# Two PSUM accumulator tiles for the second matmul in place of one, in a convolution and gated MLP kernel

## The chip, the cores and the metric

The kernel runs on one core of a Trainium2 chip. The metric is the device time of one execution in microseconds (us). The runs of the kernel before took 2665.88 to 2666.84 us, median 2666.54.

## What is computed

An input of 8 x 4096 tokens with 192 channels goes through a causal convolution of 7 taps (one softmax-normalised set of taps for each of 8 heads), and each token then through an MLP of width 2048 whose activation is a ratio of a cubic and a quadratic polynomial. Cut to what matters:

```python
# convolution: w = softmax(weight) over the 7 taps, per head
x_unf = x_pad[:, idx, :].reshape(B, S, K, H, group)
x = np.einsum('hk,bskhg->bshg', w, x_unf).reshape(B * S, D)
# MLP
h = x @ w_in                                   # 192 -> 2048
P = a[0] + a[1] * h + a[2] * h**2 + a[3] * h**3
Q = 1.0 + np.abs(b[0]) * np.abs(h) + np.abs(b[1]) * h**2
out = (P / (Q + 1e-6)) @ w_out                 # 2048 -> 192
```

## The kernel before

The 32768 tokens are cut into 64 **chunks** of 512 tokens. Each chunk passes through 8 **units**; unit k computes 256 of the 2048 hidden columns for the chunk's 512 tokens. So there are 512 units.

For a unit, PE runs gemm1 (line 512): ten matmuls of 512 columns into a PSUM tile `hp` (two buffers). ACT and DVE turn `hp` into the activation: on ACT the steps A (line 583, writes A from hp), B (586, A in place), t (579, from hp), l (593, a logarithm) and y (597, an exponential); on DVE four operations of line 305, here told apart by what they write and read: t<-t,cf,hp; g<-t,cf,y; A<-A,cf,y; g<-A,cf,g. The last leaves the unit's activation `g` in SBUF. Then PE runs gemm2 (line 521), which multiplies `g` with `w_out` and accumulates over the eight units of a chunk into PSUM. In the trace each of gemm2's fp32 matmuls is two pieces, so that a unit's gemm2 is 16 rows "op".

gemm2 comes in two **pairs**: pair 0 holds tokens 0 to 255 of the chunk, pair 1 tokens 256 to 511, each as two groups of 128. Its target is one tile `op` of [128, 4, 256] fp32, from a pool of one buffer. It is 4 KiB a partition; pair 0 writes the first 2 KiB and pair 1 the second. When a chunk's last unit is in, ACT copies the sums out in two steps of line 530 (`ob`, one for each pair), and SP sends each to memory (533).

The order of PE, ACT, DVE and POOL is written out beforehand by a planner (`plan`): a list of tasks with costs, dependencies and ranks. On PE it is gemm1 of unit k, then gemm2 of unit k-3, pair 0 and then pair 1. In the planner the first gemm2 of a chunk depends, for each pair, on the eviction of the same pair of the chunk before. The semaphore waits do not come from the planner. They are made from what each instruction reads and writes, tile by tile, and from when a pool's buffer is free again.

POOL computes the convolution of later chunks: tap by tap it scales a shifted input and adds it with an accumulating DMA; each step is tied to the end of one unit's last DVE step. The first two chunks take their convolution from PE instead. The kernel has two bodies for two kinds of coefficients; the one called with `fast` true runs here.

Of the kernel before, what the change touches and what calls it, by code (L numbers as in the profile page):

```python
# [10 lines left out]
F32 = mybir.dt.float32  # L11
# [9 lines left out]
NB, S, D = 8, 4096, 192  # L21
# [3 lines left out]
P = 128  # L25
# [179 lines left out]
def kernel(  # L205
# [13 lines left out]
    nc = tc.nc  # L219
# [12 lines left out]
    ps_o = ctx.enter_context(tc.tile_pool(name="ps_o", bufs=1, space=PS))  # L232
# [135 lines left out]
    wo_t = const.tile([P, FT, D], F32, name="wo_t")  # L368
# [8 lines left out]
    def body(fast):  # L377
# [37 lines left out]
        CP, TMP, X, H, G, O, st, last_step = {}, {}, {}, {}, {}, {}, {}, {}  # L415
# [97 lines left out]

        def gemm2(k, pair):
            c, i = divmod(k, UPC)
            if i == 0 and pair == 0:
                O[c] = ps_o.tile([P, 4, 256], F32, name="op")
            for j in range(2):
                f = 2 * i + j
                for t in (2 * pair, 2 * pair + 1):  # L520
                    nc.tensor.matmul(O[c][:, t, 0:D], lhsT=G[k][:, j, t * P:t * P + P], rhs=wo_t[:, f, :],  # L521
                                     start=(f == 0 and t % 2 == 0), stop=(f == FT - 1 and t % 2 == 1))
            if pair == 1:
                del G[k]

        def out_evac(c, pair):
            ob = opool.tile([P, 2, D], F32, name="ob")
            o = O[c][:, 2 * pair:2 * pair + 2, 0:D]
            if fast:
                nc.scalar.activation(out=ob, in_=o, func=AF.Copy, scale=K["rO"])  # L530
            else:
                nc.scalar.copy(out=ob, in_=o)
            nc.sync.dma_start(out=out_v[c, pair], in_=ob)
            if pair == 1:
                del O[c]

        def flat(t):
            return t.rearrange("p a b -> p (a b)")
# [72 lines left out]
        with tc.manual_schedule(engines={E.PE, E.Activation, E.DVE, E.Pool}):  # L611
            for kind, *which in plan(fast):
                {"w": prep, "c": conv, "xh": conv_high, "xl": conv_low, "g1": gemm1, "g2": gemm2,
                 "O": out_evac, "x": tap, "a": tap_add, "t": tap_weights, "h": high, "l": low_part}.get(kind, partial(unit, kind))(*which)
# [65 lines left out]
```

## Time and profile before

| | us |
|---|---|
| median of 3 runs | 2666.54 |
| profiled execution, its own time | 2666.89 |
| span from the first to the last instruction in it | 2664.7 |
| PE busy | 2534.2 (95%) |
| ACT busy | 2539.2 (95%) |
| DVE busy | 2516.9 (94%) |
| POOL busy | 1235.7 (46%) |
| mean granted TensorE clock | 0.995 of full speed |

Three engines are busy for nearly the whole span. A busy share is an average over the span and does not say which engine the others follow. For that one reads the chain that ended last, and then one short stretch engine by engine. A row of a timeline gives the start, the duration, the engine and line, what is written and read, and in brackets the idle time of that engine just before and what released it. An operation may start before the end of the one ahead of it on the same engine, since their first and last parts overlap.

### The profile page before, as it was taken

The page shows a single profiled execution, that of the slowest core. Times are in us where ns is not written, and L with a number is a line of the kernel's source. Part 1 is how long each engine was busy: PE and PEld are TensorE (multiplying, and loading weights), DVE is VectorE, ACT ScalarE, POOL GpSimd, SP SyncE. Part 2 cuts the span into 40 slices and gives each one's busy share as a digit, 9 for nine tenths or more (in the row PEclk, how much of TensorE's full clock was granted, in tenths as well). Part 3 has the DMA queues.
Part 4 walks back from the last instruction along what each step waited for, and adds up shares of the span by engine and source line. Part 5 has one row for each costly group of instructions (what it writes and reads, how often), then busy time and mean ns, then how long its engine had stood idle before and what let it go on. Part 6 is the DMA issues. An engine that isn't in the chain of part 4 may idle for free.

```text
span 2664.7 us, 35994 instructions
## 1 busy us (share of the span) xinstructions
PE 2534.2 (95%) x13528; PEld 2299.1 (86%) x13528; DVE 2516.9 (94%) x2160; ACT 2539.2 (95%) x2739; POOL 1235.7 (46%) x1452
## 2 busy tenths in 40 slices
PE   5999999999999999999999999999999999999998
PEld 4888888888888888888888888888888888888887
DVE  8999999999999999999999999999999999999998
ACT  7999999999999999999999999999999999999997
POOL 4454454544544444545445445454454444454530
PEclk8999999999999999999999999999999999999999
DMA  5445444445444444444544544444444444444430
GB/s 156 99 98 107 101 100 99 97 104 104 92 105 101 99 103 102 98 105 93 107 96 97 107 102 99 99 97 103 104 94 104 102 98 103 102 98 104 94 76 14
DMA packets 101721, 263.96 MB, mean 99 GB/s; under 512 B 9760, under 2 KB 44832, under 8 KB 101536
## 3 DMA queue, kind: packets, MB, share of 16 engines
q0 software_dynamic: 53568, 195.06, 38.4%
q1 hardware_dynamic: 47664, 66.04, 8.5%
q8 instruction: 108, 1.77, 0.3%
q14 instruction: 77, 0.63, 0.1%
q10 hardware_dynamic: 304, 0.46, 0.1%
HBM read 41.32 MB, written 25.17 MB: 25 GB/s over the span
## 4 chain that ended last, share of the span: by engine, by line
PE 87%; ACT 8%; DVE 2%; issue 2%; DMA 0%; POOL 0%; SPq 0%; DVEq 0%; ACTq 0%
PE op L521 50%; PE hp L512 38%; ACT l L593 2%; ACT A L586 2%; ACT ob L530 2%; ACT t L579 1%; DVE g L305 1%; DVE A L305 0%; DVE t L305 0%; ACT y L597 0%; DVE wo_t L399 0%; ACT ad L385 0%; ACT A L583 0%; PE y L434 0%; DMA wb_t<-in_wband 0%
## 5 line engine op out<-in xcount | busy, mean ns | idle before, releaser
L521 PE MATMUL op<-wo_t,g 128*128 128x192 f32 x8192 | 1424.4, 327 | 100.9 <-ACT ob L530 90.3
L521 PEld LDWEIGHTS op<-wo_t,g 128*128 128x128 f32 x8192 | 1355.6, 190 | 163.8 <-ACT ob L530 116.4
L512 PE MATMUL hp<-xh,wh_t 128*128 128x512 f32 x2048 | 872.5, 426 | 15.3 <-DVE t L305 10.6
L305 DVE SCALAR_TENSOR_TENSOR g<-t,cf,y 128x1024 f32<-128x1024 f32 x512 | 655.2, 1280 | 95.6 <-ACT y L597 78.9
L305 DVE SCALAR_TENSOR_TENSOR t<-t,cf,hp 128x1024 f32<-128x1024 f32 x512 | 653.9, 1277 | 33.8 <-ACT t L579 33.8
L305 DVE SCALAR_TENSOR_TENSOR g<-A,cf,g 128x1024 f32<-128x1024 f32 x512 | 657.0, 1283 | 1.2
L305 DVE SCALAR_TENSOR_TENSOR A<-A,cf,y 128x1024 f32<-128x1024 f32 x512 | 654.0, 1277 | 0.0
L512 PE MATMUL hp<-xh,wl_t 128*128 128x512 f32 x2048 | 633.5, 391 | 0.0
L583 ACT ACTIVATE A<-hp 128x1024 f32<-128x1024 f32 x512 | 522.1, 1020 | 49.5 <-PE hp L512 33.3
L593 ACT ACTIVATE l<-A 128x1024 f32<-128x1024 f32 x512 | 542.6, 1060 | 6.2
L586 ACT ACTIVATE A<-A 128x1024 f32<-128x1024 f32 x512 | 541.6, 1058 | 0.0
L597 ACT ACTIVATE y<-l 128x1024 f32<-128x1024 f32 x512 | 525.6, 1027 | 4.2 <-DVE xl L499 0.2
L579 ACT ACTIVATE t<-hp 128x1024 f32<-128x1024 f32 x512 | 522.0, 1020 | 0.0
L447 POOL TENSOR_SCALAR tmp<-xt,wt_t,zero 128x512 f32<-128x512 f32 x496 | 377.5, 767 | 209.3 <-DVE g L305 202.6
L512 PEld LDWEIGHTS hp<-xh,wl_t 128*128 128x128 f32 x2048 | 386.1, 189 | 86.7 <-DVE wl_t L407 0.2
L512 PEld LDWEIGHTS hp<-xh,wh_t 128*128 128x128 f32 x2048 | 387.1, 189 | 80.0 <-DVE t L305 7.3
L453 POOL DMA_DIRECT2D acc<-tmp x248 | 214.9, 867 | 414.0 <-DMA acc<-xs 369.1
L512 PE MATMUL hp<-xl,wh_t 128*128 128x512 f32 x1024 | 403.4, 394 | 0.0
L447 POOL TENSOR_SCALAR xs<-xt,wt_t,zero 128x512 f32<-128x512 f32 x248 | 188.7, 767 | 205.8 <-DVE g L305 205.8
L512 PEld LDWEIGHTS hp<-xl,wh_t 128*128 128x128 f32 x1024 | 194.2, 190 | 20.4 <-DVE xl L499 0.3
L473 POOL TENSOR_SCALAR xh<-acc,one,zero 128x1024 fp32r<-128x1024 f32 x62 | 74.2, 1198 | 251.0 <-DVE g L305 245.6
L453 POOL DMA_DIRECT2D acc<-xs x124 | 109.4, 882 | 61.3 <-DMA acc<-tmp 43.1
(57 smaller groups left out, 424.3 us busy)
## 6 DMA issues: line engine op xcount, KB each, us to landing
acc<-tmp POOLq DMA_DIRECT2D x248, 512.0 KB, 4.5
acc<-xs POOLq DMA_DIRECT2D x124, 512.0 KB, 5.2
xt<-in_xt SPq DMA_DIRECT2D x62, 518.0 KB, 4.0
out<-ob SPq DMA_DIRECT2D x128, 192.0 KB, 2.6
raw<-in_w_in SPq DMA_DIRECT2D x8, 512.0 KB, 5.7
raw<-in_w_out SPq DMA_DIRECT2D x8, 384.0 KB, 4.1
xs<-in_xa ACTq DMA_DIRECT2D x1, 324.0 KB, 4.7
xs<-in_xa SPq DMA_DIRECT2D x1, 324.0 KB, 6.5
```

The source lines that it names most:

```text
L305: return nc.vector.scalar_tensor_tensor(out=out_, in0=a, scalar=s, in1=b, op0=op0, op1=op1)
L447: ins = nc.gpsimd.tensor_scalar(to[:, n * CH:n * CH + CH], of[:, n * XA + k:n * XA + k + CH], wt_t[:, n, k:k + 1], zero, ALU.mult, ALU.add)
L453: nc.gpsimd.dma_start(out=CP[c], in_=TMP.pop((c, k)), accum_op=ALU.add)
L473: ins = nc.gpsimd.tensor_scalar(X[c][0].rearrange("p a b -> p (a b)"), CP[c], one, zero, ALU.mult, ALU.add)
L512: nc.tensor.matmul(H[k][:, j, :], lhsT=w[:, i, part, j, :], rhs=x, start=(n == 0), stop=(n == 4))
L521: nc.tensor.matmul(O[c][:, t, 0:D], lhsT=G[k][:, j, t * P:t * P + P], rhs=wo_t[:, f, :], start=(f == 0 and t % 2 == 0), stop=(f == FT - 1 ...
L530: nc.scalar.activation(out=ob, in_=o, func=AF.Copy, scale=K["rO"])
L579: nc.scalar.activation(out=work_tile(k, "t"), in_=h, func=AF.Square, scale=K["rt"], bias=1.0)
L583: nc.scalar.activation(out=work_tile(k, "A"), in_=h, func=AF.Abs, scale=K["rA"])
L586: nc.scalar.activation(out=s["A"], in_=s["A"], func=AF.Square, bias=1.0)
L593: nc.scalar.activation(out=work_tile(k, "l"), in_=s["A"], func=AF.Ln, scale=K["rL"], bias=1.0)
L597: nc.scalar.activation(out=work_tile(k, "y"), in_=s["l"], func=AF.Exp, scale=-1.0)
```

## The change

`op` becomes two tiles, `op0` and `op1`, one for each pair, each of [128, 2, 256] fp32 (2 KiB a partition), and each with one buffer under a name of its own. The matmuls and the two copies on ACT do the same work on the same amount of PSUM.

```diff
         def gemm2(k, pair):
             c, i = divmod(k, UPC)
-            if i == 0 and pair == 0:
-                O[c] = ps_o.tile([P, 4, 256], F32, name="op")
+            if i == 0:
+                O[c, pair] = ps_o.tile([P, 2, 256], F32, name=f"op{pair}")
             for j in range(2):
                 f = 2 * i + j
                 for t in (2 * pair, 2 * pair + 1):
-                    nc.tensor.matmul(O[c][:, t, 0:D], lhsT=G[k][:, j, t * P:t * P + P], rhs=wo_t[:, f, :],
+                    nc.tensor.matmul(O[c, pair][:, t % 2, 0:D], lhsT=G[k][:, j, t * P:t * P + P], rhs=wo_t[:, f, :],
                                      start=(f == 0 and t % 2 == 0), stop=(f == FT - 1 and t % 2 == 1))
...
         def out_evac(c, pair):
             ob = opool.tile([P, 2, D], F32, name="ob")
-            o = O[c][:, 2 * pair:2 * pair + 2, 0:D]
+            o = O.pop((c, pair))[:, :, 0:D]
...
-            if pair == 1:
-                del O[c]
```

The planner is not touched, and no engine's order changes. What changes are the waits of two instructions at each chunk boundary. On ACT, around the two evictions of a chunk (the number behind a name is that of the buffer or tile; `DMAHW` is the transfer that frees `ob`), before:

```order
L583 ACTIVATE A_2609<-hp_2589 128x1024 [waits PE_49]
L597 ACTIVATE y_2613<-l_2602 128x1024 [waits DVE_49,Activation_49]
L530 ACTIVATE ob_2619<-op_2347 128x384 [waits DMAHW2_49,PE_49]
L586 ACTIVATE A_2609<-A_2609 128x1024 [waits Activation_49]
L579 ACTIVATE t_2640<-hp_2589 128x1024
L593 ACTIVATE l_2643<-A_2609 128x1024 [waits Activation_49]
L530 ACTIVATE ob_2651<-op_2347 128x384 [waits DMAHW3_49]
L597 ACTIVATE y_2654<-l_2643 128x1024 [waits DVE_49,Activation_49]
```

and now:

```order
L581 ACTIVATE A_2616<-hp_2596 128x1024 [waits PE_49]
L595 ACTIVATE y_2620<-l_2609 128x1024 [waits DVE_49,Activation_49]
L530 ACTIVATE ob_2626<-op0_2353 128x384 [waits DMAHW2_49,PE_49]
L584 ACTIVATE A_2616<-A_2616 128x1024 [waits Activation_49]
L577 ACTIVATE t_2647<-hp_2596 128x1024
L591 ACTIVATE l_2650<-A_2616 128x1024 [waits Activation_49]
L530 ACTIVATE ob_2658<-op1_2365 128x384 [waits DMAHW3_49,PE_49]
L595 ACTIVATE y_2661<-l_2650 128x1024 [waits DVE_49,Activation_49]
```

Each eviction now reads a tile of its own and waits for PE itself; before, the first waited for PE on behalf of both. On PE, around the first gemm2 of the next chunk, before:

```order
L512 MATMUL hp_2629<-xl_2368,wh_t_182 128x512
L512 MATMUL hp_2629<-xh_2367,wh_t_182 128x512
L512 MATMUL hp_2629<-xh_2367,wl_t_183 128x512 x2
L521 MATMUL op_2646<-wo_t_184,g_2587 128x192 [waits DVE_49,PE_49,Activation_49]
L521 MATMUL op_2646<-wo_t_184,g_2587 128x192 x7
L512 MATMUL hp_2668<-xh_2367,wh_t_182 128x512 [waits DVE_49]
```

and now:

```order
L512 MATMUL hp_2636<-xl_2375,wh_t_182 128x512
L512 MATMUL hp_2636<-xh_2374,wh_t_182 128x512
L512 MATMUL hp_2636<-xh_2374,wl_t_183 128x512 x2
L521 MATMUL op0_2653<-wo_t_184,g_2594 128x192 [waits DVE_49,Activation_49]
L521 MATMUL op0_2653<-wo_t_184,g_2594 128x192 x3
L521 MATMUL op1_2664<-wo_t_184,g_2594 128x192 [waits Activation_49]
L521 MATMUL op1_2664<-wo_t_184,g_2594 128x192 x3
L512 MATMUL hp_2676<-xh_2374,wh_t_182 128x512 [waits DVE_49]
```

The wait for ACT that stood once, ahead of all eight matmuls, stands twice now, ahead of each pair's four.

## Rows read from the trace of the kernel before

**Rows 1.** The page, part 4: the chain that ended last, by engine.

```profile
PE 87%; ACT 8%; DVE 2%; issue 2%; DMA 0%; POOL 0%; SPq 0%; DVEq 0%; ACTq 0%
```

**Rows 2.** Busy time by stretch: one chunk, behind the late boundary at 256, behind a boundary.

```profile
core 0: us, PE busy (x) PEld busy (x) DVE busy (x) ACT busy (x) POOL busy (x), PEclk, DMA share, GB/s
...
1218.73:1259.55 40.82, 39.34 (x210) 35.73 (x209) 38.71 (x33) 39.30 (x43) 19.56 (x24) 1.00 0.48 100
...
258.00:260.30 2.30, 2.30 (x10) 2.30 (x8) 2.30 (x3) 2.30 (x3) 1.55 (x2) 0.51 0.00 0
...
1240.00:1274.00 34.00, 34.00 (x183) 31.14 (x182) 32.42 (x28) 33.00 (x35) 15.87 (x19) 1.00 0.48 94
```

**Rows 3.** The chain in order of time at a chunk boundary: start, us, what.

```profile
1228.79 2.28 PE hp L512 x10
1231.07 2.61 PE op L521 x16
...
1237.43 2.87 PE op L521 x16
1240.30 2.31 PE hp L512 x10
1242.61 2.60 PE op L521 x16
```

**Rows 4.** Waits: total us, times, longest us.

```profile
PE op L521 <- ACT ob L530: 90.3, 62, 2.4
```

**Rows 5.** Timeline of PE at that boundary.

```profile
1230.91 2.76 PE L521 MATMUL op<-wo_t,g 128*128 128x192 f32 x16
1233.37 0.53 PE L512 MATMUL hp<-xh,wh_t 128*128 128x512 f32 x1
...
1237.43 2.87 PE L521 MATMUL op<-wo_t,g 128*128 128x192 f32 x16 [1.48 <-ACT ob L530]
```

**Rows 6.** Timeline of ACT: an early boundary, this boundary, the end of this chunk.

```profile
134.28 1.05 ACT L593 ACTIVATE l<-A 128x1024 f32<-128x1024 f32 x1
135.22 1.02 ACT L583 ACTIVATE A<-hp 128x1024 f32<-128x1024 f32 x1
...
1232.02 1.02 ACT L597 ACTIVATE y<-l 128x1024 f32<-128x1024 f32 x1
1233.70 0.49 ACT L530 ACTIVATE ob<-op 128x384 f32<-128x384 f32 x1 [0.66 <-PE op L521]
...
1236.89 0.49 ACT L530 ACTIVATE ob<-op 128x384 f32<-128x384 f32 x1
1237.26 1.04 ACT L597 ACTIVATE y<-l 128x1024 f32<-128x1024 f32 x1
1238.20 1.03 ACT L583 ACTIVATE A<-hp 128x1024 f32<-128x1024 f32 x1
...
1241.13 1.06 ACT L593 ACTIVATE l<-A 128x1024 f32<-128x1024 f32 x1
1242.64 1.02 ACT L583 ACTIVATE A<-hp 128x1024 f32<-128x1024 f32 x1 [0.45 <-PE hp L512]
...
1270.84 1.06 ACT L593 ACTIVATE l<-A 128x1024 f32<-128x1024 f32 x1
1271.92 1.02 ACT L583 ACTIVATE A<-hp 128x1024 f32<-128x1024 f32 x1
```

**Rows 7.** Timeline of PE and of all engines at two earlier boundaries.

```profile
174.34 2.87 PE L521 MATMUL op<-wo_t,g 128*128 128x192 f32 x16 [0.57 <-ACT ob L530]
...
256.01 4.55 PE L521 MATMUL op<-wo_t,g 128*128 128x192 f32 x16 [2.43 <-ACT ob L530]
```

**Rows 8.** Timeline of ACT at the end of the program.

```profile
2658.62 0.87 ACT L530 ACTIVATE ob<-op 128x384 f32<-128x384 f32 x2 [7.49 <-PE op L521]
```

**Rows 9.** Line 530's instructions on ACT's queue: count, ns min/median/max.

```profile
L530 ACTq EVENT_SEMAPHORE  x63: 17/17/17, 129.0 to 2650.1; - x63
```

**Rows 10.** Timeline of DVE at the boundary.

```profile
1236.09 1.28 DVE L305 SCALAR_TENSOR_TENSOR t<-t,cf,hp 128x1024 f32<-128x1024 f32 x1 [0.53 <-ACT t L579]
...
1244.62 1.28 DVE L305 SCALAR_TENSOR_TENSOR g<-t,cf,y 128x1024 f32<-128x1024 f32 x1 [1.28 <-ACT y L597]
```

## The prediction

> **What bounds the kernel now.** I read the chain of waits first. It says which engine the end hangs on: 87% of the span is TensorE work [rows 1]. Busy shares alone would not tell this, since in one chunk PE, ACT and DVE are busy 39.34, 39.30 and 38.71 of 40.82 us [rows 2]. Then the chain in order of time, around one chunk boundary. Away from the boundary it alternates gemm1 of a unit (hp, 2.28 us) with gemm2 of the unit three earlier (op, 2.60), with nothing between: 4.88 us a unit, and 8 x 4.88 = 39.04 us a chunk. [...] At the boundary the chain leaves PE: op ends at 1233.68, the next op starts only at 1237.43, and what lies between on the chain is ACT [rows 3]. The waits view gives the place: PE waited 62 times for the eviction "ob", 90.3 us in all [rows 4].
>
> Call the new chunk's units 0 to 7 and the evictions of the old chunk O0 (pair 0) and O1 (pair 1). PE's timeline [rows 5]: gemm2 of the old unit 7 from 1230.91, gemm1 of unit 3 from 1233.37, then 1.48 idle, then gemm2 of unit 0 at 1237.43. ACT's timeline [rows 6]: it issues y at 1232.02, then is idle 0.66 waiting for PE, O0 at 1233.70, three steps, O1 at 1236.89 for 0.49, so done at 1237.38. PE goes 0.05 after that. So two waits are in a row: O0 waits for all 16 matmul pieces of the old gemm2 (they end at 1230.91 + 2.76 = 1233.67, and O0 starts 0.03 later), which pushes O1 back, and the new chunk's first matmul waits for O1, though it writes only pair 0's half.
>
> **What the change does to O0.** It has to wait for pair 0's 8 pieces only. These end half of 2.60 before the others, at about 1233.67 - 1.30 = 1232.37. ACT has its queue slot after y: an op behind y starts 0.94 after it (1237.26 to 1238.20 [rows 6]), so O0 goes at 1232.96, now bound by ACT's own order and not by PE. Gain on ACT: 0.74, and everything queued behind O0 moves up with it, O1 to 1236.15, done at 1236.64.
>
> **What it does to PE.** Pair 0's matmuls of unit 0 need O0 alone (done at 1233.45); gemm1 of unit 3 leaves PE at 1233.37 + 4.88 - 2.46 = 1235.79 (2.46 is gemm2's start to the next start, 1230.91 to 1233.37 [rows 5]). So pair 0 goes at once. Pair 1's follow 1.30 later, at 1237.09, and need O1, done at 1236.64: 0.45 to spare. Both halves of the change are needed: with O1 at its old 1237.38 pair 1 would still stop for 0.3.
>
> **The sum for a boundary**, on the chain [rows 3]: from the end of the old op (1233.68) to the end of the gemm1 behind the stall (1242.61) are 8.93 us; without the stall it is hp + op + hp = 2.28 + 2.60 + 2.28 = 7.16. So 1.77 a boundary: the wait itself, and 0.27 + 0.03 by which op and hp run longer behind it.
>
> **How many boundaries.** Of the 62 waits, 58 are of this kind. Three early ones idle only 0.57 in place of 1.48 (the row at 174.34), so they are worth 1.77 - 0.91 = 0.86 each, 2.6 in all. [...] It is worth 1.77 + 0.95 + 1.68 = 4.40. The sum: 58 x 1.77 + 2.6 + 4.4 = 109.7 us. I know the 58 from the total: 58 x 1.48 + 3 x 0.57 + 2.43 = 90.0, against the 90.3 of the waits view [rows 4].
>
> **At the end** the two last evictions stand in a row for 0.87 behind the last matmul [rows 8]; O0 now goes while pair 1 still runs, which saves about 0.4. Against that the last boundary is not followed by 39 us of PE work but by the drain through DVE, so its 1.77 may shrink, by 0 to 1.77; I take 0.4, and the two cancel.
>
> **What is added.** One more wait on O1, 63 in the span. The semaphore instruction that O0 already has there takes 17 ns [rows 9]: 1.1 us in all on ACT, and on the path only if ACT bounds. Nothing is added on PE, DVE, POOL or SP, whose order stays, and no DMA; the out transfers of O0 are issued 0.74 earlier.
>
> **Where the cover could fail.** At 39.04 a chunk the others must still fit. DVE is busy 38.71 [rows 2]. Its waits of 0.53 and 1.28 at the boundary [rows 10] come from ACT's late t and from PE's stall and shrink with them. ACT is busy 39.30, above 39.04, but that counts ops end to end: an op behind an unblocked l starts 0.94 after it (134.28 to 135.22), while l itself runs 1.05, so 0.11 overlap. In this chunk six starts are blocked and lose that overlap: O0, and five A that wait for their gemm1 (first 1241.13 to 1242.64, last 1270.84 to 1271.92) [rows 6]. Without the blocks ACT needs 39.30 - 6 x 0.11 = 38.6, or 0.4 under PE. The O0 and O1 work sets ACT back by up to 1.5 us against PE at unit 3 (A at 1238.20 - 0.74 = 1237.46; its gemm1 ends on the chain at 1233.68 + 2.28 = 1235.96), and one unit later by 0.5 (A at 1241.13 - 0.74 + 0.94 = 1241.33, against 1235.96 + 4.88 = 1240.84). PE's nearest need of that late work is gemm1 of unit 4, which reuses the buffer that DVE's t of unit 2 reads: due at 1233.37 + 4.88 = 1238.25, and t, even unmoved, ends at 1236.09 + 1.28 = 1237.37 [rows 10]. POOL is busy 19.56 of 40.82 and follows DVE's g.
>
> [...] The row shows O0 starting 0.03 after the last piece of both pairs [rows 5, 6], so the wait of before goes by the whole tile. [...]
>
> **Rivals.**
> 1. *PE closes every boundary* (forecast). 2666.9 - 109.7 = 2557.2 on the profiled execution; that one is 0.35 above the median of the runs, so about 2557. Its own range is 2554 to 2562 (the tail, and the one clock fall, of which some may stay). Chance 0.81.
> 2. *ACT or DVE takes over.* If ACT's 39.30 is its floor, a chunk costs 0.26 more than PE's 39.04, over 62 chunks 16 us: about 2573. For it: the busy row. Against: the 0.94 start behind an l. Chance 0.10.
> 3. *Half of it*: O0 stays where it is (PE signals the pairs no earlier in effect), pair 1 stops 0.3 at each boundary and pays the restart of 0.30 again: 0.6 of 1.77 stays, 62 x 0.6 = 37: about 2594. For it: only 0.45 to spare. Against: O0 has 0.6 between pair 0's end and its slot. Chance 0.05.
> 4. *Nothing changes*: the waits of before already go by the half, O0 is late for another reason (the buffer ob, or ACT's queue), and the split frees nothing: 2666.5. Against it stand the 0.66 that ACT idles for PE and the 0.03 behind both pairs' last piece [rows 6]. Chance 0.02. [...]
> 5. *Slower.* Now PE may stop in the middle of a gemm2. If ACT, with O0 and O1 both queued among its steps, slips until O1 comes as late for pair 1 as it came at 256.01 for pair 0, each boundary is like that one: 2.43 idle and half the clock behind it, 4.40 in place of 1.77, so 62 x 2.63 = 163 more: about 2830. It is slower than before from where a boundary costs over 1.77, that is where ACT needs over 40.82 a chunk, against the 38.6 above. Chance 0.02.
>
> **How the numbers follow.** Faster by over 0.2% (5 us, about what a measurement of this kernel can tell from no change): cases 1 to 3, 0.96. Within: 0.02. Slower: 0.02. The range reaches from the best of case 1, where PE never waits and the tail gains too, to the price of case 2: 2554 to 2574, which holds 0.9 of the cases as priced and some less for what I mis-sized.
>
> **What would show it.** Right: PE's wait for ob gone or under 0.1 a boundary; chunk period 39.04; O0 about 0.94 behind y; no clock fall near 256. Wrong: PE idle in the middle of an op run (case 3), PE waiting at hp for DVE's t or a gemm2 for g, with ACT idle nowhere (case 2), or a period still of 40.82 (case 4).

## The result, and the profile after

The changed kernel takes 2556.94 us (median of 4 runs, 2556.78 to 2557.57); the kernel before, measured beside it, 2666.61 (4 runs, 2665.88 to 2666.84). The ratio is 0.959, with a 95% interval of 0.9573 to 0.9606. The forecast was about 2557, in a range of 2554 to 2574. The profiled execution of the changed kernel took 2557.57 us, its span is 2555.5, and the numbers below are read in it.

The page of the changed kernel, part 1 (busy time, share of the span, instructions) and part 4 (the chain that ended last):

```profile
PE 2516.3 (98%) x13528; PEld 2304.0 (90%) x13528; DVE 2495.9 (98%) x2160; ACT 2512.8 (98%) x2739; POOL 1244.8 (49%) x1452
...
PE 68%; ACT 19%; DVE 8%; issue 5%; DMA 0%; DVEq 0%; SPq 0%; ACTq 0%
```

PE's share of the chain was 87% before [rows 1] and is 68% now. That doesn't mean that ACT has taken over. Three engines are now busy for 98% of the span, so for much of it the chain can be followed back through any of them at no difference; which engine decides is seen in a stretch, not in this line. Busy time by stretch, one chunk of the changed kernel (columns as in [rows 2]):

```profile
core 0: us, PE busy (x) PEld busy (x) DVE busy (x) ACT busy (x) POOL busy (x), PEclk, DMA share, GB/s
1210.69:1249.73 39.04, 39.04 (x210) 35.82 (x210) 38.37 (x33) 38.86 (x43) 19.70 (x23) 1.00 0.52 105
```

The chunk takes 39.04 us where it took 40.82, and PE is busy in all of it. ACT fell from 39.30 to 38.86 and DVE from 38.71 to 38.37 with the same work. The chain of the changed kernel around a chunk boundary (start, us, what) now alternates without a gap:

```profile
1223.03 2.60 PE op L521 x16
1225.63 2.28 PE hp L512 x10
1227.91 2.60 PE op L521 x16
1230.51 2.28 PE hp L512 x10
```

The stretch from 1233.68 to 1237.43, which ran through ACT [rows 3], is gone, and so is the entry "PE op L521 <- ACT ob L530" of the waits [rows 4]: no such line is left in the view. PE's timeline at this boundary (start, us, engine, line, operation, and in brackets the idle time before it and what ended it):

```profile
1222.87 2.76 PE L521 MATMUL op<-wo_t,g 128*128 128x192 f32 x16
1225.33 0.53 PE L512 MATMUL hp<-xh,wh_t 128*128 128x512 f32 x1
...
1227.75 2.76 PE L521 MATMUL op<-wo_t,g 128*128 128x192 f32 x16
```

and ACT's:

```profile
1223.99 1.02 ACT L595 ACTIVATE y<-l 128x1024 f32<-128x1024 f32 x1
1224.94 0.48 ACT L530 ACTIVATE ob<-op 128x384 f32<-128x384 f32 x1
...
1228.11 0.50 ACT L530 ACTIVATE ob<-op 128x384 f32<-128x384 f32 x1
1228.48 1.05 ACT L595 ACTIVATE y<-l 128x1024 f32<-128x1024 f32 x1
```

O0 (1224.94) starts while PE is still in the old chunk's last gemm2, which ends at 1222.87 + 2.76 = 1225.63; before, it started 0.03 behind both pairs [rows 5, 6]. O1 (1228.11 to 1228.61) is evicted while PE already writes the new chunk's pair 0, from 1227.75. PE's gemm2 of unit 0 carries no idle time in brackets, and takes 2.76 like any other.

### The profile page after: what moved, and what is told of

Its sections match the earlier page's. It is cut to its first block, busy times and chain, and to the rows that moved or that the text cites. A ratio compares the mean times of both kernels' runs of the same rounds, so it can differ in the third digit from the quotient of the medians.

```text
span 2555.5 us, 36057 instructions
## 1 busy us (share of the span) xinstructions
PE 2516.3 (98%) x13528; PEld 2304.0 (90%) x13528; DVE 2495.9 (98%) x2160; ACT 2512.8 (98%) x2739; POOL 1244.8 (49%) x1452
## 3 DMA queue, kind: packets, MB, share of 16 engines
q8 instruction: 108, 1.77, 0.3%
## 4 chain that ended last, share of the span: by engine, by line
PE 68%; ACT 19%; DVE 8%; issue 5%; DMA 0%; DVEq 0%; SPq 0%; ACTq 0%
PE op L521 36%; PE hp L512 32%; ACT y L595 4%; ACT A L584 4%; ACT A L581 3%; ACT t L577 3%; ACT l L591 3%; DVE A L305 2%; DVE t L305 2%; DVE g L305 2%; ACT ob L530 1%; ACT ad L385 0%; ACT ad L387 0%; PE y L434 0%; DVE wo_t L399 0%
## 5 line engine op out<-in xcount | busy, mean ns | idle before, releaser
L521 PE MATMUL op<-wo_t,g 128*128 128x192 f32 x8192 | 1418.0, 326 | 10.3 <-DVE g L305 10.3
L521 PEld LDWEIGHTS op<-wo_t,g 128*128 128x128 f32 x8192 | 1360.6, 190 | 51.5 <-issue 9.2
L305 DVE SCALAR_TENSOR_TENSOR g<-t,cf,y 128x1024 f32<-128x1024 f32 x512 | 654.1, 1278 | 38.6 <-ACT y L595 34.7
L447 POOL TENSOR_SCALAR tmp<-xt,wt_t,zero 128x512 f32<-128x512 f32 x496 | 384.0, 788 | 191.3 <-DVE g L305 184.6
L453 POOL DMA_DIRECT2D acc<-xs x124 | 109.7, 884 | 67.3 <-DMA acc<-tmp 48.5
```

What stands on the lines that cost most here:

```text
L305: return nc.vector.scalar_tensor_tensor(out=out_, in0=a, scalar=s, in1=b, op0=op0, op1=op1)
L447: ins = nc.gpsimd.tensor_scalar(to[:, n * CH:n * CH + CH], of[:, n * XA + k:n * XA + k + CH], wt_t[:, n, k:k + 1], zero, ALU.mult, ALU.add)
L453: nc.gpsimd.dma_start(out=CP[c], in_=TMP.pop((c, k)), accum_op=ALU.add)
L521: nc.tensor.matmul(O[c, pair][:, t % 2, 0:D], lhsT=G[k][:, j, t * P:t * P + P], rhs=wo_t[:, f, :], start=(f == 0 and t % 2 == 0), stop=(f ...
```

## Experiments

All seven kernels keep the order of every engine as the changed kernel has it, except where the text says that O1 moves or that matmuls are left out.

**both_waits: two tiles, with the waits of one.** The tiles stay apart, and two dependencies are added by hand: O0 waits for pair 1's last matmul, and the new chunk's first matmul waits for O1. `last_mm` and `evac` hold the instructions; `evicted_first` only writes O1 ahead of that matmul in the program, so that it can be named; no engine's order moves by it.

```diff
+        def behind(ins, other):
+            tc.add_manual_dep(ins.ins, other.name,
+                              mybir.DependencyInfo(mybir.DependencyClass.Sync, mybir.DependencyReason.DATA),
+                              reason="as with one tile")
...
+                    if c and f == 0 and t == 0:
+                        behind(ins, evac[c - 1, 1])
+            last_mm[c, pair] = ins.ins
...
+            evac[c, pair] = ins.ins
+            if pair == 0:
+                behind(ins, last_mm[c, 1])
...
-            for kind, *which in plan(fast):
+            for kind, *which in evicted_first(plan(fast)):
```

> Two tiles, but with both waits of before put back. Theory (the gain is made of these two waits and of nothing else, such as where the tiles lie in PSUM): the time of before, 2666.6 us, with 1.48 of PE idle at each boundary and the fallen clock at 256. Rival (the split itself, by bank or by address, gives part of the gain): a time between 2557 and 2666.

Measured: 2665.33 us (10 runs, 2664.66 to 2666.2), ratio to the kernel before 0.9998 (0.9989 to 1.0008). PE's timeline and the waits of both_waits:

```profile
1277.78 2.87 PE L547 MATMUL op<-wo_t,g 128*128 128x192 f32 x16 [1.49 <-ACT ob L559]
```

```profile
PE op L547 <- ACT ob L559: 90.3, 62, 2.4
```

These are the rows of before within a hundredth: 1.48 idle [rows 5], and 90.3 us in 62 waits [rows 4]. So the whole gain comes from these two waits. That the accumulators are two tiles in place of one costs or gains nothing beside them that an interval of 0.1% could tell.

**o0_late: only O0's wait is put back.** O0 waits for both pairs; the new chunk's pairs each wait for their own eviction.

```diff
+            last_mm[c, pair] = ins.ins
...
+            if pair == 0:
+                behind(ins, last_mm[c, 1])
```

> The changed kernel (2556.9 us) with one wait put back: O0 waits for the last matmul of pair 1 again; PE still waits pair by pair. Theory (two waits in a row, ACT's order sets O1): O0 goes back to 0.03 behind the last piece of both pairs, so O1 ends 0.74 later, 0.3 after pair 1 of the new chunk is due; with the restart of 0.3 each boundary loses 0.6, and the time is about 2594 us. Rival (only PE's wait for both evictions cost time before, O0's late start did not): the time stays at 2557.

Measured: 2586.83 us (4 runs, 2586.21 to 2587.9), ratio 0.9704 (0.9688 to 0.972). ACT's timeline and PE's of o0_late at one boundary:

```profile
1236.50 1.02 ACT L605 ACTIVATE y<-l 128x1024 f32<-128x1024 f32 x1
1238.17 0.49 ACT L537 ACTIVATE ob<-op 128x384 f32<-128x384 f32 x1 [0.65 <-PE op L527]
...
1241.36 0.49 ACT L537 ACTIVATE ob<-op 128x384 f32<-128x384 f32 x1
```

```profile
1240.26 1.46 PE L527 MATMUL op<-wo_t,g 128*128 128x192 f32 x8
1241.90 1.57 PE L527 MATMUL op<-wo_t,g 128*128 128x192 f32 x8 [0.19 <-ACT ob L537]
```

ACT is idle 0.65 ahead of O0, as in [rows 6], and PE stops in the middle of a gemm2, as the prediction described the case where half of the wait stays. The size was off. Pair 1 was due at 1240.26 + 1.30 = 1241.56 and started at 1241.90, 0.34 late, which is what was expected; but a boundary lost 0.47, not 0.6 (from the start of one gemm1 to that of the next are 5.33 to 5.34 us here in place of 4.88, and 39 of the 57 chunks from 6 to 62 lose another 0.03 to 0.04 a unit later). In before the start was 1237.43 - 1235.79 = 1.64 late and the boundary cost 1.77, so PE loses 0.13 on top of a late start. The 0.30 that I added goes on top of the idle time as the row prints it (1.48), which is shorter than the delay. I had taken the delay and added what belongs to the idle time.

**pe_both: only the matmul's wait is put back.** O0 is free of pair 1; the new chunk's pair 0 waits for O1.

```diff
+                    if c and f == 0 and t == 0:
+                        behind(ins, evac[c - 1, 1])
...
-            for kind, *which in plan(fast):
+            for kind, *which in evicted_first(plan(fast)):
```

> The changed kernel with the other wait put back: the first matmul of pair 0 of a chunk waits for O1; O0 still goes early. Theory: O1 ends at the early time, 0.85 after pair 0 is due, so a boundary loses 0.74 less than the 1.77 of before, 1.03, and the time is about 2557 + 62 x 1.0 = 2619 us, with PE idle 0.74 at each boundary. Rival (O0's late start was the whole cost): 2557.

Measured: 2617.49 us (4 runs, 2617.3 to 2618.64), ratio 0.9819 (0.9803 to 0.9836). ACT's timeline and PE's of pe_both:

```profile
1249.58 1.02 ACT L625 ACTIVATE y<-l 128x1024 f32<-128x1024 f32 x1
1250.52 0.48 ACT L559 ACTIVATE ob<-op 128x384 f32<-128x384 f32 x1
...
1253.69 0.50 ACT L559 ACTIVATE ob<-op 128x384 f32<-128x384 f32 x1
```

```profile
1254.25 2.87 PE L547 MATMUL op<-wo_t,g 128*128 128x192 f32 x16 [0.74 <-ACT ob L559]
```

O0 stands 0.94 behind y, so ACT gained its 0.74; PE then still waits for O1, 0.74 of the 1.48 it idled before. A boundary costs 5.89 - 4.88 = 1.01 here, and up to 0.04 more a unit later; the chunks take 40.05 to 40.09.

The two waits don't add up. Alone, O0's costs 2586.83 - 2556.94 = 29.9 us and the matmul's 60.6; together they cost 108.4. The spare time says why: with only O0's wait, 0.45 of the 0.74 that ACT comes late is hidden by the 1.30 in which PE does pair 0 (0.74 - 0.45, + 0.05 from O1's end at 1241.85 to PE's start at 1241.90 in o0_late, = 0.34 late, + 0.13 = 0.47). With both, nothing hides it: 1.01 + 0.74 = 1.75 a boundary, near the 1.77 measured.

**o1_later: O1 one ACT step later.** The changed kernel with O1 moved behind the y that follows it on ACT (`second_later` moves it, and writes it ahead of the matmuls that need it); no wait is added.

```diff
-            for kind, *which in plan(fast):
+            for kind, *which in second_later(plan(fast)):
```

> The changed kernel with O1 moved one step back in ACT's order, behind the y (in the first chunks the l or A) that followed it; the work is the same. Theory (pair 1 of a new chunk has 0.45 to spare, and PE is the bound): O1 ends 0.94 later, 0.5 after pair 1 is due, and with the restart of 0.3 a boundary loses 0.8: about 2557 + 60 x 0.8 = 2605 us. Rival (the spare time is larger, or ACT and DVE catch up): 2557.

Measured: 2605.55 us (4 runs, 2605.01 to 2607.18), ratio 0.9774 (0.9758 to 0.9791). ACT's timeline and PE's of o1_later:

```profile
1247.91 1.07 ACT L623 ACTIVATE l<-A 128x1024 f32<-128x1024 f32 x1
1249.00 1.03 ACT L627 ACTIVATE y<-l 128x1024 f32<-128x1024 f32 x1
1249.97 0.47 ACT L562 ACTIVATE ob<-op 128x384 f32<-128x384 f32 x1
```

```profile
1248.49 1.46 PE L553 MATMUL op<-wo_t,g 128*128 128x192 f32 x8
1250.49 1.57 PE L553 MATMUL op<-wo_t,g 128*128 128x192 f32 x8 [0.54 <-ACT ob L562]
```

Pair 1 was due at 1248.49 + 1.30 = 1249.79 and started 0.70 late; with the 0.13 the boundary should cost 0.83, and a chunk takes 39.87, 0.83 over 39.04. So the spare time of the changed kernel is real and small: one ACT step more ahead of O1 costs 48.6 us. That the time came out as expected is partly luck, since two errors cancel. O1 ends 1250.44 - 1248.49 = 1.95 behind the start of pair 0, where it was 1228.61 - 1227.75 = 0.86 in the changed kernel: 1.09 later and not 0.94, because y now follows l directly and starts 1.09 behind it (1247.91 to 1249.00). Against that the late start costs 0.13 on top and not 0.3.

**less_pe: how near is the next bound?** The changed kernel without one of gemm1's five terms, the low weights times the third piece of the input, so that PE has less to do and ACT the same.

```diff
-            terms = [(wh_t, 0, xhA), (wh_t, 0, xlA), (wh_t, 1, xB), (wl_t, 0, xhA), (wl_t, 1, xB)]
+            terms = [(wh_t, 0, xhA), (wh_t, 0, xlA), (wh_t, 1, xB), (wl_t, 0, xhA)]
...
-                    nc.tensor.matmul(H[k][:, j, :], lhsT=w[:, i, part, j, :], rhs=x, start=(n == 0), stop=(n == 4))
+                    nc.tensor.matmul(H[k][:, j, :], lhsT=w[:, i, part, j, :], rhs=x, start=(n == 0), stop=(n == 3))
```

> The changed kernel with the last of gemm1's five terms left out (the low part of the weights times the third input piece), which takes two matmuls of 0.228 us from each unit: PE needs 4.42 a unit, 35.4 us a chunk. It measures what bounds next. Theory (ACT without its blocked starts needs 38.6 a chunk, DVE 38.2): the chunk falls from 39.04 to 38.6 to 38.8, about 2557 - 62 x 0.35 = 2535 us, with ACT or DVE gapless. Rival 2 of the prediction (ACT's busy time of 39.3 is its floor): the time stays at 2557 or above. If PE alone bounded: 2557 - 512 x 0.456 = 2324.

Measured: 2543.19 us (4 runs, 2540.57 to 2545.22), ratio 0.9535 (0.9519 to 0.955). Busy time by stretch, one chunk of less_pe:

```profile
1243.82:1282.62 38.80, 37.26 (x192) 32.62 (x193) 38.26 (x33) 38.64 (x43) 19.62 (x23) 1.00 0.51 106
```

A fifth of gemm1 is gone, 0.46 of 4.88 us a unit, but a chunk falls only from 39.04 to 38.80. PE now has idle time, and ACT's steps follow one another with hardly a gap. So ACT needs 38.8 a chunk, not the 39.30 that its busy row of before shows [rows 2] and not the 38.6 that I worked out either: it lies 0.24 under PE, not 0.4. Its busy time, 38.64, is what was worked out. What was left out are the other 0.16: five steps of this chunk read what the step just ahead of them on ACT writes, and these start 0.03 behind its end, where others start before it (the first A below at 1245.41, 0.11 ahead of the end of the t before it, 1244.50 + 1.02). ACT's timeline of less_pe shows the first of them (1245.41 + 1.06 = 1246.47, and l starts at 1246.50):

```profile
1245.41 1.06 ACT L584 ACTIVATE A<-A 128x1024 f32<-128x1024 f32 x1
1246.50 1.06 ACT L591 ACTIVATE l<-A 128x1024 f32<-128x1024 f32 x1
```

The 38.8 refutes the rival in which ACT sets 39.3, and it says that the changed kernel can't gain more than about 15 us (62 x 0.24) by PE alone. A need of 38.8 gives 2556.94 - 62 x 0.24 = 2542 us, near the measured time; the 2535 expected would take 38.69 a chunk.

**less_pe_one_tile: the same term left out of the kernel before.** The diff is that of less_pe, on the kernel with one shared tile.

> The kernel of before, one shared tile, with the same term left out of gemm1. Theory: with PE off the path, PE's wait for O1 costs nothing by itself and the change is worth little: the time is within 10 us of that of less_pe. Rival (the two waits in a row hold ACT and DVE too, through O0's late start): most of the 1.77 a boundary stays, about 100 us above less_pe.

Measured: 2625.98 us (4 runs, 2624.93 to 2626.73), ratio 0.9847 (0.9831 to 0.9863): 83 us above less_pe. Busy time by stretch, two neighbouring chunks of less_pe_one_tile and a piece behind the boundary of each (the column behind POOL is the granted clock):

```profile
1239.72:1280.28 40.56, 37.94 (x195) 34.22 (x194) 38.27 (x33) 38.76 (x43) 19.60 (x23) 0.96 0.50 102
1280.28:1319.19 38.91, 36.29 (x194) 32.65 (x193) 38.25 (x33) 38.75 (x43) 19.59 (x23) 1.00 0.51 105
1260.00:1263.00 3.00, 3.00 (x10) 2.90 (x10) 3.00 (x3) 2.97 (x4) 2.70 (x4) 0.50 0.00 0
1300.00:1302.00 2.00, 2.00 (x13) 1.96 (x13) 2.00 (x3) 2.00 (x3) 1.65 (x2) 1.00 0.24 74
```

PE's timeline of less_pe_one_tile at these two boundaries:

```profile
1258.34 4.13 PE L521 MATMUL op<-wo_t,g 128*128 128x192 f32 x16 [2.50 <-ACT ob L530]
...
1298.89 2.87 PE L521 MATMUL op<-wo_t,g 128*128 128x192 f32 x16 [2.50 <-ACT ob L530]
```

The chunks are of two kinds. In one the wait of 2.50 us costs almost nothing: 38.91 against the 38.80 of less_pe, because ACT sets the pace and PE has time to wait (busy 38.75 and 36.29 of the 38.91). In the other the granted clock is at 0.50 from 1260 to 1263, behind the same 2.50 us of idle time, and the chunk takes about 40.57. Of the chunks 6 to 62, 45 are of the slow kind and 12 of the fast one: 45 x 1.67 + 57 x 0.11 = 81 of the 83 us. So the theory that a PE with time to spare loses nothing by the wait holds for the wait itself, and misses what the clock does behind it: 83 us above less_pe, where at most 10 were expected. The rival's 100 us is nearer, but not by its mechanism: O0 isn't late here, it starts 0.95 behind y (1253.67 to 1254.62). What ACT waits for in the slow chunks is the gemm1 behind the fallen clock, in the waits of less_pe_one_tile:

```profile
ACT A L583 <- PE hp L512: 79.8, 48, 2.7
```

In less_pe this wait is 4.6 us in 3.

**both_o1_later: the price of the slower case.** both_waits with O1 one ACT step later, so that PE idles at each boundary about as long as before's late one at 256.01 [rows 7].

```diff
-            for kind, *which in evicted_first(plan(fast)):
+            for kind, *which in second_later(plan(fast)):
```

> Two tiles with both waits of before put back, and O1 one step later in ACT's order: PE idles about 1.48 + 0.94 = 2.4 us at each boundary, as long as at the one boundary at 256 before which TensorE's clock fell. Theory (such an idle time brings the clock down each time): a boundary costs 4.40 in place of 1.77, about 2666 + 62 x 2.6 = 2830 us, and the granted clock of the run falls. Rival (the fall at 256 hung on something else, or on when the idle time came): only the added wait, 2666 + 62 x 0.94 = 2725 us, or between the two when some boundaries fall and others do not.

Measured: 2788.38 us (4 runs, 2786.72 to 2789.59), ratio 1.0455 (1.0438 to 1.0473). PE's timeline and the busy time by stretch of both_o1_later at two boundaries:

```profile
307.92 2.87 PE L559 MATMUL op<-wo_t,g 128*128 128x192 f32 x16 [2.58 <-ACT ob L571]
...
349.81 4.55 PE L559 MATMUL op<-wo_t,g 128*128 128x192 f32 x16 [2.57 <-ACT ob L571]
```

```profile
308.00:312.00 4.00, 4.00 (x22) 3.75 (x23) 4.00 (x4) 3.70 (x4) 3.57 (x4) 1.00 0.15 49
352.00:354.00 2.00, 2.00 (x9) 2.00 (x8) 2.00 (x3) 1.58 (x2) 1.59 (x2) 0.50 0.04 8
```

The idle time is 2.57 to 2.58 us at both, yet the clock stays at 1.00 behind the first and is at 0.50 behind the second, where the 16 pieces take 4.55 in place of 2.87, just as at 256.01. Of the chunks 6 to 62, 31 take 43.6 us and 26 take 41.9. A boundary with a fall costs 43.58 - 39.04 = 4.54 and one without 2.85. The idle time is longer than the 2.4 expected, since O1 comes 1.09 later here too, as in o1_later. The result lies between the two times expected, since neither "every boundary" nor "none" is right.

## Why the prediction was right

**The place and the two waits.** Right, and shown: both_waits has the time of before (0.9998), and each wait alone has a price of its own. That the two stand in a row, so that both halves of the change are needed, was argued in the prediction and is what the 29.9, 60.6 and 108.4 us say.

**O0 bound by ACT's order.** Forecast 0.94 behind y; it is 1223.99 to 1224.94, 0.95.

**Pair 1's spare time.** Forecast 0.45. In the changed kernel pair 1 is due at 1227.75 + 1.30 = 1229.05 and O1 is done at 1228.61: 0.44. It is 0.44 at 55 of the 63 boundaries, but not at the late one, as shown below.

**The sum.** From the start of gemm1 of unit 8 to that of unit 511, a stretch that holds every chunk boundary, before took 2566.98 us (75.64 to 2642.62) and the changed kernel 2457.21 (76.10 to 2533.31): 109.77 less, against 109.7 worked out. The start-up is 0.46 longer and the end 0.1, which makes 109.2, the difference of the spans. (The start-up lies ahead of the first boundary, and takes 75.3 to 77.0 us in the seven kernels here that have all of gemm1, so a hit to 0.1 us is partly luck.) The single terms are each a little off: a steady boundary gave 40.82 - 39.04 = 1.78, and of the 4.40 at the late boundary, the one at 256.01, some 0.5 stayed, since its chunk takes 39.50. (Before, that chunk took 43.46 us, from 236.36 to 279.82 by its gemm1 starts: 4.42 over 39.04, against the 4.40 in the sum.) Its clock fall, to 0.51 [rows 2], is gone. PE's and ACT's timelines of the changed kernel there, and the granted clock of the stretches around it,

```profile
251.29 3.01 PE L521 MATMUL op<-wo_t,g 128*128 128x192 f32 x16
...
252.18 0.50 ACT L530 ACTIVATE ob<-op 128x384 f32<-128x384 f32 x1
```

```profile
251.00:254.00 3.00, 3.00 (x18) 2.65 (x17) 3.00 (x3) 3.00 (x5) 0.96 (x2) 1.00 1.04 213
254.00:257.00 3.00, 3.00 (x15) 2.38 (x15) 3.00 (x4) 3.00 (x4) 1.53 (x2) 1.00 0.07 25
```

show a gemm2 of 3.01 with no idle time ahead of it, against 4.55 behind 2.43 [rows 7], at a clock of 1.00. The 3.01 in place of 2.76 is a wait that stayed. At this early boundary ACT has four steps between O0 and O1 and not three, so O1 ends at 252.18 + 0.50 = 252.68, when pair 1 was due at 251.29 + 1.30 = 252.59. Pair 1 started at 252.73, 0.14 late, a stop too short for the waits view to list; it is the case of half the wait, at one boundary.

**The end.** Forecast: a gain of 0.4 and a loss of 0.4. ACT's timeline of the changed kernel at the end:

```profile
2548.85 0.49 ACT L530 ACTIVATE ob<-op 128x384 f32<-128x384 f32 x1 [6.96 <-PE op L521]
2550.15 0.49 ACT L530 ACTIVATE ob<-op 128x384 f32<-128x384 f32 x1 [0.81 <-PE op L521]
```

The two evictions are now 1.30 apart, each behind its own pair, where they stood together behind both [rows 8]. From the last matmul's end to that of O1 are 0.52 in place of 0.91, so the gain of 0.4 is there. The end as a whole is 0.1 longer all the same. Counted from the start of gemm1 of unit 511, the last matmul ends 0.84 later. Some 0.3 of this is the drain through DVE, the loss that was forecast at 0.4: gemm2 of unit 510 waits for its g and starts at 2542.97 - 2533.31 = 9.66, where before it was 2652.01 - 2642.62 = 9.39. The rest stands behind a clock fall that the end of before doesn't have and that was not forecast (PE's timeline, and the granted clock in the column behind POOL):

```profile
2542.97 7.15 PE L521 MATMUL op<-wo_t,g 128*128 128x192 f32 x32 [1.89 <-DVE g L305]
```

```profile
2545.00:2548.00 3.00, 3.00 (x11) 3.00 (x11) 1.58 (x2) 0.00 (x0) 0.00 (x0) 0.55 0.04 8
```

Against that, some 0.35 less pass from the end of O1 to the end of the span. So the two terms were about right, and that the end as a whole came out at nothing is partly luck.

**What is added.** Forecast: 63 more semaphore instructions of 17 ns on ACT. The instructions of line 530 in the changed kernel:

```profile
L530 ACTq EVENT_SEMAPHORE  x126: 17/17/17, 129.5 to 2548.9; - x126
```

126 in place of the 63 of [rows 9], and as PE is busy in all of a chunk, they cost nothing that shows.

**ACT and DVE as the next bound.** The direction was right, the size a little too kind. ACT's need is 38.8 a chunk by less_pe, where I had 38.6: the idle time between steps that read one another's results was left out. DVE's waits at the boundary shrank as forecast, from 1.28 [rows 10] to 0.61 in DVE's timeline of the changed kernel:

```profile
1235.29 1.28 DVE L305 SCALAR_TENSOR_TENSOR g<-t,cf,y 128x1024 f32<-128x1024 f32 x1 [0.61 <-ACT y L595]
```

It is now 34.7 us in 58 waits, about 0.6 at a boundary, caught up again before PE needs the g: PE waits for none in these chunks.

**The rivals.** That ACT or DVE takes over (2573) is refuted by less_pe. That half of the wait stays (2594) was a sound mechanism with its price too high: o0_late, which is that case, takes 2586.8, since the restart was counted at 0.30 where 0.13 belongs. That nothing changes fell with the result. In the changed kernel ACT reads pair 1's tile from 1228.11 while PE writes pair 0's from 1227.75. The wait of before was one that the program set, by the whole tile, and both_waits shows its full price with the accumulators in separate tiles: 2665.33 us, against 2556.94 without it. The slower case had the right price for a boundary with a clock fall (4.40 forecast, 4.54 measured at a somewhat longer idle time) and the wrong assumption that every such boundary has one.

## What to carry to other kernels

Look at who waits for a buffer as a whole while using a part of it: ACT and PE were held here by the tile, where with a tile for each half ACT reads one (from 1228.11) while PE writes the other (from 1227.75), and the waits view shows it as one small wait repeated at every boundary (62 waits, 90.3 us). Follow such a wait back one step more, because the engine that is waited for may itself be late by the same tile; the two delays then stand in a row, and undoing one alone leaves a part of the loss (here 29.9 or 60.6 of 108.4 us). Before counting on the gain, work out how much spare time is left behind it and which engine is next: here 0.44 us at a boundary, and 0.24 us a chunk under PE.

## What the runs showed of the chip

The clock fell behind some idle times and not behind others of the same length, in the same execution. In both_o1_later PE did the same work ahead of each boundary and idled 2.57 to 2.58 us, and the granted clock was at 0.50 behind 31 of 57 and at 1.00 behind the others; in less_pe_one_tile, with 2.46 to 2.50 us in nearly every chunk, behind 45 of 57. The falls are not scattered: in both_o1_later chunks with and without one alternate, and after every eleven or thirteen chunks two with a fall stand in a row. In less_pe_one_tile every fourth or fifth chunk is without. No run shows what sets this beat. The length of the idle time alone doesn't order the cases either: a fall came behind 1.89 us at the end of the changed kernel, and behind 1.90 in PE's timeline of less_pe_one_tile,

```profile
292.78 4.54 PE L521 MATMUL op<-wo_t,g 128*128 128x192 f32 x16 [1.90 <-ACT ob L530]
```

with a granted clock of 0.61 from 293.0 to 296.5, where 2.57 had no fall in 26 chunks of both_o1_later. What is shown: behind the 1.48 us of before and both_waits no steady boundary had a fall, and behind 2.57 us the price of one more ACT step was 1.07 us at some boundaries (2.85 - 1.78) and 2.76 at others.
